# A weight converter that runs four steps further ahead in a fused attention and expert-layer kernel

## The chip, the cores and the metric

One core of one Trainium2 chip. The metric is the device time of one execution in microseconds: 653.36 us, the median of three runs (652.16 to 654.46).

## The reference

Three layers, one behind the other, all in float32:

```
attention: q, k, v of (2, 8, 576, 64); scores = q k^T / 8, masked per head:
           heads 0-3 see the last 32 positions, heads 4-7 every 32nd position
           attn = softmax(scores); x = attn v, as (1152, 512)
dense:     x = ((x @ w1) * (x @ w2)) @ w3 @ w_out      (512 -> 1024 -> 1024 -> 512)
experts:   p = probs / (sum(probs) + 1e-9); out = sum over 4 experts e of
           p[:, e] * (relu(x @ u1[e]) @ u2[e])         (512 -> 1024 -> 512)
```

The dense weights w1, w2, w3 and w_out arrive as float64, 8 bytes an element.

## The kernel before, in words

**Products.** Each factor is split into a high and a low part, and every product is three matmuls (`mm3`, L256 to L258): high by high, low by high, high by low. A weight chunk is thus of use only when both `w_hi` and `w_lo` of it exist; the third matmul of a block is the first that reads `w_lo`.

**Weight conversion.** The 20 chunks of the dense weights (8 of w1 and w2 together, 4 of w_out, 8 of w3) come as 64-bit words and are turned into float32 by integer work on the two 32-bit halves (class `Chunk`, L124 on): `round_up` (ScalarE, L136) works on the low words, `magnitude` (ScalarE, L144; for chunk 0 VectorE, L142) takes the high words without their sign into a tile `t`, then `clamp` (L147), `shift` (L150), `sign` (L153) and `add` (L157) on VectorE; `add` joins the low words and its method issues the load of the next raw chunk on SyncE's queue, with further loads hung on some of them (`rest_loads`: the third carries v of batch 1, the fourth its q and k, the fifth more of v). Last, `split_hi` (ScalarE, L164) writes w_hi and `split_lo` (VectorE, L174) writes w_lo. There are two raw buffers and two `t` tiles, so chunk n+2 is loaded when `add` of chunk n is done.

**Who hands the steps out.** The generator `work()` (L201) lists these steps in order and yields between them; `advance(n)` takes n of them. The engines work their queues in the order in which the program issues instructions, so where `advance` stands between other work is where the steps stand in each engine's queue. `split_hi` waits, by not being issued, while `live`, the count of occupied tiles of the pool for values and weights, is over 14. `need(chunk)` takes steps until that chunk is split.

**Stages.** Attention of batch 0 is nine steps of `attend(0, s)` with `advance` of 2, 3, 1 and 1 steps behind steps 4 to 7, which is just chunk 0 as far as its w_lo, and some idle matmuls (`keep_warm`). Then come 32 units, `run_unit()`: batch 0, then batch 1; in each, 8 feature groups (ft), each needing weight chunk ft, by 2 halves of the tokens. A unit is two accumulators of 12 matmuls (`ab_block`): the first is copied by ScalarE (L476), the second multiplied by that copy on VectorE (L478), and behind each stands `advance(1)`. Attention steps of batch 1 (`attend(1, s)`, nine of them) stand behind units 2, 4, 5, 7, 8, 10, 11, 13 and 14, and free value tiles as they go. Batch 1 uses the same eight chunks and frees them one by one. Behind the units: w3 times w_out in eight tiles (`wc_tile`, accumulators `wc_acc`), each needing one more chunk, with `advance(5)` behind each; x3, the dense layer's output; and the experts.

**Pools.** Five PSUM banks serve all accumulators except the scores and the experts' products, which have three of their own.

Of the kernel before, what the change touches and what calls it, by code (L numbers as in the profile page):

```python
# [42 lines left out]
def kernel(  # L43
# [157 lines left out]
    def work():  # L201


        wide = stream[:20]
        wide[0].round_up()
        wide[0].magnitude()
        yield True
        before = None
        for c, after in zip(wide, wide[1:] + [None]):
            if before:  # L210
                while live > 14:
                    yield False
                before.split_hi()
            c.clamp()
            yield True
            if before:
                before.split_lo()
            c.shift()
            yield True
            c.sign()  # L220
            yield True
            if after:
                after.round_up()
            c.add()
            yield True
            before = c
            if c is wide[0]:
                c.split_hi()
                yield True
                c.split_lo()  # L230
                yield True
                before = None
            if after:
                after.magnitude()
        while live > 14:
            yield False
        before.split_hi()
        yield True
        before.split_lo()
        yield True  # L240
        for w in c_e:
            yield from w.work()

    worker = work()

    def advance(n=1):

        return all([next(worker, False) for _ in range(n)])
# [363 lines left out]
    class Step:  # L612
# [22 lines left out]
        def add(self, out, acc, b):  # L635
            nc.vector.tensor_tensor(out=out, in0=acc, in1=b, op=ALU.add)  # L636

        def first(self, work):

            n = self.half.n  # L640
# [6 lines left out]
            self.product(b, "s2", "t2")  # L647
            self.add(u2, b, u1)
            work(1)
            self.product(c, "s3", "t3")  # L650
            self.add(u3, c, u2)
# [69 lines left out]
    with tc.manual_schedule():  # L721
# [42 lines left out]
        def attend(b, s):  # L764

            nonlocal live
            chunk = chunks[b]
            n = len(chunk)
            if s == 0:
                chunk[0].scores()  # L770
            if s + 1 < n:
                chunk[s + 1].scores()
            if s < n:
                chunk[s].maxima()
                chunk[s].exps()
            if 1 <= s <= n:
                chunk[s - 1].sums()
                chunk[s - 1].normalise()
            if 3 <= s:
                c = chunk[s - 3]  # L780
                c.pv()
                c.put()
                c.put_lo()
                if c.g == 0 or c.c > 0:
                    live -= 1
            if 2 <= s < n + 2:
                chunk[s - 2].transposes()
                chunk[s - 2].evac(nc.scalar.copy)

        for s in range(9):  # L790
            attend(0, s)
            advance({4: 2, 5: 3, 6: 1, 7: 1}.get(s, 0))
            keep_warm({4: 20, 5: 14, 6: 12, 8: 16}.get(s, 8))
        steps = iter(range(9))
        while done < 16:
            run_unit()
# [13 lines left out]
        for it in range(8):  # L810
# [9 lines left out]
            if i is not None:  # L820
                c = wc[i]
# [4 lines left out]
        c = None  # L826
# [134 lines left out]
```

## Time and profile before

| | |
|---|---|
| median of three runs | 653.36 us (652.16 to 654.46) |
| the profiled execution | 652.93 us, of which its span is 651.1 |
| TensorE busy | 626.3 us, 96% of the span |
| VectorE busy | 454.3 us, 70% |
| ScalarE busy | 265.0 us, 41% |
| mean granted TensorE clock | 0.990 |

Engines are named PE (TensorE matmuls), PEld (its weight loads), DVE (VectorE), ACT (ScalarE), POOL (GpSimd) and SP (SyncE). Times in a timeline are from the first instruction of the span. What stands in square brackets behind an instruction is the time that its engine was idle just before it, and what ended that. Back-to-back instructions overlap by about a tenth of a microsecond in their records. The clock is given as a share of full speed.

### The profile page before, as it was taken

The page shows a single profiled execution, that of the slowest core. Times are in us where ns is not written, and L with a number is a line of the kernel's source. Part 1 is how long each engine was busy: PE and PEld are TensorE (multiplying, and loading weights), DVE is VectorE, ACT ScalarE, POOL GpSimd, SP SyncE. Part 2 cuts the span into 40 slices and gives each one's busy share as a digit, 9 for nine tenths or more (in the row PEclk, how much of TensorE's full clock was granted, in tenths as well). Part 3 has the DMA queues.
Part 4 walks back from the last instruction along what each step waited for, and adds up shares of the span by engine and source line. Part 5 has one row for each costly group of instructions (what it writes and reads, how often), then busy time and mean ns, then how long its engine had stood idle before and what let it go on. Part 6 is the DMA issues. An engine that isn't in the chain of part 4 may idle for free.

```text
span 651.1 us, 11452 instructions
## 1 busy us (share of the span) xinstructions
PE 626.3 (96%) x4706; PEld 571.1 (88%) x4706; DVE 454.3 (70%) x819; ACT 265.0 (41%) x455; POOL 4.9 (1%) x25
## 2 busy tenths in 40 slices
PE   8879896999998999999999999999899999999997
PEld 6778796999886999999899989998798989899996
DVE  5956797489877512677787787797786575664843
ACT  3634464466664412433343343334434333333321
POOL 2000000000000000000000000000000000000000
PEclk9989899999999999999999999999999999999999
DMA  8854323234333311143355335543568564656311
GB/s 261 301 163 125 119 72 125 66 99 158 133 130 129 130 65 65 35 150 139 130 193 182 143 134 190 182 142 130 193 214 319 195 225 163 211 188 246 131 65 65
DMA packets 28727, 99.45 MB, mean 153 GB/s; under 512 B 2652, under 2 KB 6740, under 8 KB 26116
## 3 DMA queue, kind: packets, MB, share of 16 engines
q1 hardware_dynamic: 28132, 98.14, 42.8%
q8 instruction: 37, 0.61, 0.4%
q10 hardware_dynamic: 544, 0.59, 0.3%
q14 instruction: 14, 0.11, 0.0%
HBM read 79.58 MB, written 19.14 MB: 152 GB/s over the span
## 4 chain that ended last, share of the span: by engine, by line
PE 75%; DVE 11%; DMA 6%; ACT 5%; issue 2%; SPq 0%; DVEq 0%; ACTq 0%
PE g_acc L256 10%; PE g_acc L257 10%; PE g_acc L258 10%; PE m_a L256 4%; PE m_a L258 4%; PE m_a L257 4%; DMA raw<-in_w3T_dram 3%; PE ab_acc L258 3%; PE ab_acc L256 3%; PE ab_acc L257 3%; PE x_acc L256 3%; PE x_acc L257 3%; PE x_acc L258 3%; PE m_b L257 3%; PE m_c L256 3%; PE m_c L257 3%
## 5 line engine op out<-in xcount | busy, mean ns | idle before, releaser
L630 ACT ACTIVATE h_hi<-u 128x320 fp32r<-128x320 f32 (+1 forms) x128 | 57.0, 446 | 188.4 <-DVE u L636 188.4
L256 PE MATMUL g_acc<-w_hi,h_hi 128*128 128x512 f32 (+1 forms) x296 | 114.3, 386 | 0.0
L257 PE MATMUL g_acc<-w_lo,h_hi 128*128 128x512 f32 (+1 forms) x296 | 114.2, 386 | 0.0
L258 PE MATMUL g_acc<-w_hi,h_lo 128*128 128x512 f32 (+1 forms) x296 | 113.7, 384 | 0.0
L256 PE MATMUL ab_acc<-x_hi,w_hi 128*128 128x288 f32 x256 | 79.5, 311 | 7.9 <-ACT w_hi L164 7.9
L258 PE MATMUL ab_acc<-x_hi,w_lo 128*128 128x288 f32 x256 | 78.7, 307 | 4.8 <-DVE w_lo L174 4.8
L257 PE MATMUL ab_acc<-x_lo,w_hi 128*128 128x288 f32 x256 | 77.9, 304 | 0.0
L636 DVE TENSOR_TENSOR u<-m_b,u 128x320 f32<-128x320 f32 (+1 forms) x96 | 40.8, 453 | 53.1 <-PE m_b L258 51.4
L569 DVE TENSOR_TENSOR w_lo<-raw,w_hi 128x768 fp32r<-128x768 f32 x64 | 69.4, 1085 | 12.0 <-ACT w_hi L567 11.9
L258 PEld LDWEIGHTS g_acc<-w_hi,h_lo 128*128 128x128 f32 x296 | 55.6, 188 | 11.6
L256 PEld LDWEIGHTS g_acc<-w_hi,h_hi 128*128 128x128 f32 x296 | 55.8, 188 | 8.0
L257 PEld LDWEIGHTS g_acc<-w_lo,h_hi 128*128 128x128 f32 x296 | 55.7, 188 | 7.6
L632 DVE SCALAR_TENSOR_TENSOR h_lo<-u,h_hi 128x320 fp32r<-128x320 f32 (+1 forms) x128 | 57.8, 451 | 3.5 <-ACT h_hi L630 1.4
L567 ACT CAST w_hi<-raw 128x768 fp32r<-128x768 f32 x64 | 59.9, 936 | 0.0
L256 PEld LDWEIGHTS ab_acc<-x_hi,w_hi 128*128 128x128 f32 x256 | 50.6, 197 | 9.3 <-ACT w_hi L164 8.6
L258 PEld LDWEIGHTS ab_acc<-x_hi,w_lo 128*128 128x128 f32 x256 | 50.4, 197 | 6.5 <-DVE w_lo L174 6.3
L257 PEld LDWEIGHTS ab_acc<-x_lo,w_hi 128*128 128x128 f32 x256 | 50.6, 198 | 0.0
L257 PE MATMUL m_b<-b_t,s_hi 128*128 128x320 f32 (+1 forms) x128 | 37.9, 296 | 0.0
L636 DVE TENSOR_TENSOR u<-m_a,u 128x320 f32<-128x320 f32 (+1 forms) x64 | 28.9, 452 | 11.6 <-PE m_a L258 11.6
L569 DVE TENSOR_TENSOR s_lo<-raw,s_hi 128x1024 fp32r<-128x1024 f32 x16 | 19.6, 1225 | 23.2 <-ACT s_hi L567 23.2
L636 DVE TENSOR_TENSOR u<-m_c,u 128x320 f32<-128x320 f32 (+1 forms) x64 | 29.0, 453 | 4.6 <-PE m_c L258 3.8
L136 ACT ACTIVATE raw<-raw 128x1024 int32<-128x1024 uint32 x20 | 23.4, 1170 | 20.7 <-DMA raw<-in_w3T_dram 18.3
(153 smaller groups left out, 1388.2 us busy)
## 6 DMA issues: line engine op xcount, KB each, us to landing
raw<-in_e_dram SPq DMA_DIRECT2D x32, 1024.0 KB
raw<-in_w_dram SPq DMA_DIRECT2D x8, 1024.0 KB
raw<-in_w3T_dram SPq DMA_DIRECT2D x8, 1024.0 KB
stored<-s_hi SPq DMA_DIRECT2D x16, 512.0 KB
stored<-s_lo SPq DMA_DIRECT2D x16, 512.0 KB
s_hi<-stored SPq DMA_DIRECT2D x16, 512.0 KB
s_lo<-stored SPq DMA_DIRECT2D x16, 512.0 KB
raw<-in_w_out_dram SPq DMA_DIRECT2D x4, 1024.0 KB
```

Source lines behind the costliest of these rows:

```text
L136: nc.scalar.activation(self.low, self.low.bitcast(U32), AF.Copy, scale=2.0 ** -29)
L256: mm(acc, lh, rh, start=first, stop=False)
L257: mm(acc, lh, rl, start=False, stop=False)
L258: mm(acc, ll, rh, start=False, stop=last)
L567: nc.scalar.copy(dst[0], src)
L569: nc.vector.tensor_tensor(out=dst[1], in0=src, in1=dst[0].bitcast(F32), op=ALU.subtract)
L630: nc.scalar.activation(hi, src, AF.Relu)
L632: nc.vector.scalar_tensor_tensor(out=lo, in0=src, scalar=0.0, in1=hi.bitcast(F32), op0=ALU.max, op1=ALU.subtract)
L636: nc.vector.tensor_tensor(out=out, in0=acc, in1=b, op=ALU.add)
```

## The change

Two edits. In `work()`, the `round_up` of chunk 1 moves from ahead of `add` of chunk 0 to behind `split_hi` of chunk 0, in the step that issues that; its `magnitude` stays where it was. For every later chunk `magnitude` moves from behind the yield that follows `add` of the chunk before to directly behind `round_up`, ahead of that `add`. In the main program four more steps are handed out between the attention of batch 0 and the first unit: `magnitude` and `clamp` of chunk 1; `shift`; `sign`; `round_up` and `magnitude` of chunk 2 with `add` of chunk 1 and the loads behind it.

```
             c.sign()
             yield True
-            if after:
+            if after and c is not wide[0]:
                 after.round_up()
+                after.magnitude()
             c.add()
             yield True
             before = c
             if c is wide[0]:
                 c.split_hi()
+                after.round_up()
                 yield True
                 c.split_lo()
                 yield True
                 before = None
-            if after:
                 after.magnitude()
...
             attend(0, s)
             advance({4: 2, 5: 3, 6: 1, 7: 1}.get(s, 0))
             keep_warm({4: 20, 5: 14, 6: 12, 8: 16}.get(s, 8))
+        advance(4)
         steps = iter(range(9))
         while done < 16:
             run_unit()
```

## Rows read from the trace of the kernel before

**Rows 1.** The profile's page, busy us (share of the span) and instructions of each engine.
```profile
PE 626.3 (96%) x4706; PEld 571.1 (88%) x4706; DVE 454.3 (70%) x819; ACT 265.0 (41%) x455; POOL 4.9 (1%) x25
```

**Rows 2.** TensorE's waits, 215 to 651: us in total, times, longest.
```profile
PE m_a L256 <- ACT u L646: 0.9, 1, 0.9
```

**Rows 3.** TensorE's waits, 33 to 109.
```profile
PE ab_acc L256 <- ACT w_hi L164: 6.3, 3, 3.3
PE ab_acc L258 <- DVE w_lo L174: 3.9, 5, 1.5
```

**Rows 4.** TensorE's timeline at two waits: start, us, line, form [idle before].
```profile
45.15 0.61 PE L256 MATMUL ab_acc<-x_hi,w_hi 128*128 128x288 f32 x1 [3.31 <-ACT w_hi L164]
46.41 0.61 PE L258 MATMUL ab_acc<-x_hi,w_lo 128*128 128x288 f32 x1 [0.41 <-DVE w_lo L174]
...
67.32 0.40 PE L256 MATMUL ab_acc<-x_hi,w_hi 128*128 128x288 f32 x1 [2.05 <-ACT w_hi L164]
```

**Rows 5.** Stretches: length, PE, PEld, DVE, ACT, POOL busy; clock; DMA share, GB/s.
```profile
36.03:39.36 3.33, 3.33 (x28) 3.33 (x26) 2.77 (x4) 1.58 (x3) 0.00 (x0) 1.00 0.00 0
33.40:109.15 75.75, 65.49 (x844) 60.33 (x842) 56.25 (x94) 35.52 (x60) 0.23 (x2) 0.93 0.37 121
46.81:51.61 4.80, 4.80 (x21) 4.80 (x21) 1.37 (x2) 1.44 (x2) 0.00 (x0) 0.50 0.52 196
68.61:72.05 3.44, 3.44 (x15) 3.44 (x16) 1.77 (x2) 0.67 (x2) 0.00 (x0) 0.52 0.03 5
80.00:98.00 18.00, 17.29 (x225) 15.91 (x217) 17.44 (x32) 10.90 (x23) 0.00 (x0) 1.00 0.22 65
113.14:116.50 3.36, 3.36 (x16) 3.36 (x15) 1.27 (x2) 1.43 (x2) 0.00 (x0) 0.50 0.02 5
```

**Rows 6.** TensorE's waits, 109 to 126.
```profile
PE ab_acc L256 <- ACT w_hi L164: 1.6, 1, 1.6
PE ab_acc L258 <- DVE w_lo L174: 0.9, 1, 0.9
```

**Rows 7.** ScalarE's timeline at the end of batch 0's attention.
```profile
27.70 1.05 ACT L164 CAST w_hi<-t 128x1024 fp32r<-128x1024 f32 x1 [1.06 <-DVE t L157]
28.65 0.90 ACT L437 CAST x_hi<-o 128x216 fp32r<-128x216 f32 x2
29.94 0.59 ACT L389 COPY pT<-tp 128x512 f32<-128x512 f32 x1 [0.39 <-PE tp L384]
31.60 0.68 ACT L437 CAST x_hi<-o 128x108 fp32r<-128x108 f32 x4 [1.07 <-PE o L410]
```

**Rows 8.** ScalarE's instructions by line, 33.4 to 109.15: busy us, mean ns; idle before.
```profile
L144 ACT ACTIVATE t<-raw 128x1024 f32<-128x1024 f32 x8 | 9.1, 1137 | 0.0
L136 ACT ACTIVATE raw<-raw 128x1024 int32<-128x1024 uint32 x7 | 8.2, 1166 | 0.0
```

**Rows 9.** VectorE's instructions by line, the same stretch.
```profile
L153 DVE SCALAR_TENSOR_TENSOR t<-raw,t 128x1024 int32<-128x1024 int32 x7 | 8.6, 1222 | 0.1
L157 DVE CUSTOM_DVE_ANT_0 t<-raw,t 128x2048 uint16<-128x2048 uint16 x7 | 8.5, 1216 | 0.0
...
L147 DVE TENSOR_SCALAR t<-t 128x1024 f32<-128x1024 f32 x7 | 4.9, 694 | 8.6 <-ACT t L144 8.6
```

**Rows 10.** A stretch, columns as in rows 5.
```profile
41.55:50.00 8.45, 4.72 (x38) 4.21 (x28) 4.70 (x6) 3.25 (x5) 0.00 (x0) 0.69 0.77 263
```

**Rows 11.** The chain that ended last, in order of time: start, us, what.
```profile
165.69 5.87 DMA raw<-in_w3T_dram
```

**Rows 12.** VectorE's waits, 126 to 206.
```profile
DVE t L147 <- ACT t L144: 6.7, 8, 1.6
```

**Rows 13.** TensorE's waits, 130 to 240.
```profile
PE wc_acc L256 <- ACT w_hi L164: 1.3, 1, 1.3
PE wc_acc L258 <- DVE w_lo L174: 0.8, 1, 0.8
```

**Rows 14.** ScalarE's timeline in batch 1.
```profile
128.18 0.40 ACT L476 COPY ab<-ab_acc 128x288 f32<-128x288 f32 x1 [0.62 <-PE ab_acc L258]
```

More of the change, by code (lines that the diff above doesn't have):

```diff
@@ L221, in work @@
             yield True
-            if after:
+            if after and c is not wide[0]:
                 after.round_up()
+                after.magnitude()
             c.add()
@@ L228, in work @@
                 c.split_hi()
+                after.round_up()
                 yield True
@@ L232, in work @@
                 before = None
-            if after:
                 after.magnitude()
@@ L793 @@
             keep_warm({4: 20, 5: 14, 6: 12, 8: 16}.get(s, 8))
+        advance(4)
         steps = iter(range(9))
```

## The prediction

> **What bounds the kernel now.** I read the page's busy line first, then TensorE's waits stage by stage, its timeline at the waits, and last the other engines' queues at the same places. TensorE is busy 626.3 us (96%) [rows 1], so what can be won is some 25 us of waits and whatever it runs at the low clock. Behind 215 us there is next to nothing: the longest wait there is 0.9 us [rows 2]. The place to look is the first projection of batch 0, from the end of its attention (33.4) to the end of batch 1's (109.15). There TensorE waits 6.3 us in 3 waits for w_hi and 3.9 us in 5 for w_lo [rows 3]: at the turn from one eighth of the features (ft) to the next, the weight chunk is not yet converted. The largest are 3.31 + 0.41 us before ft 1 and, for w_hi alone, 2.05 before ft 3 [rows 4]. Behind each of these two the granted clock is 0.50 and 0.52, the lower of the two levels (1.2 GHz) [rows 5]. One more wait of this kind stands at ft 7, 1.6 + 0.9 us [rows 6], also with a stretch at 0.50 behind it [rows 5].
>
> Why it waits is in the order of the code. Two converter steps go with each half of a batch's tokens, so the chunk for ft k is split in the last unit of ft k-1, and its w_lo stands on VectorE behind the product of that unit's last accumulator. TensorE has always finished before. For ft 1 it is worse, since none of chunk 1's four steps is out before the first block.
>
> **The change part by part.**
>
> *The round_up of chunk 1 goes behind split_hi of chunk 0.* ScalarE runs that split at 27.70, the next x_hi copies at 28.65, the pT copy at 29.94 for 0.59 us [rows 7]. A round_up has a mean of 1.17 us [rows 8], some 1.07 back to back. With it in between, the x_hi copies begin at about 29.7 and, at 0.90, the pT copy at 30.6 or a little later, so the last attention product, and ft 0 behind it, begin 0.6 us later. The slot that the round_up leaves, earlier in the same loop, gives nothing back: the VectorE chain there does not wait for it. Cost 0.6; between 0, if the 16 idle matmuls ahead of ft 0 took it up, which they can't as they stand in TensorE's queue behind that product, and the whole 1.17.
>
> *Four steps before the first block.* They issue on ScalarE a magnitude (1.14), a round_up (1.17) and another magnitude; on VectorE clamp 0.69, shift (an estimate: as the clamp), sign 1.22 and add 1.22 [rows 8, 9]; and behind the add on SyncE the load of raw chunk 3 and, since that load carries them, the q and k of batch 1. ScalarE is through with the attention's last copies at 31.60 + 0.68 [rows 7], 32.9 with the shift of 0.6. So: magnitude to 34.0, clamp, shift, sign, add to 37.8, w_hi to 38.9. Clamp 2 and the first product come in VectorE's queue ahead of w_lo, which is done at about 40.1. TensorE came to these weights at 45.15 - 3.31 = 41.84 [rows 4], now 42.4. Both are there 2 us before. Behind the waiting instructions, ScalarE's first copy of an accumulator (wanted at 35.6) stands until about 36.5 and VectorE's first product until 38.7; that holds two of five PSUM banks, and TensorE needs the first of them again only at 44. No cost. The wait of 3.7 us goes, and with it the slow stretch: 20 matmuls start from 46.81 to 51.61 (21 are counted, one reaches in), 0.24 us each. At full clock 25 start in 3.33 us (28 counted, three reach in), 0.133 each; 20 would take 2.7 us, so 2.1 us go too [rows 5].
>
> *The lead stays.* From now on each chunk is split in the first unit of the ft before, a whole unit earlier (24 matmuls of 0.133, 3.2 us, and an attention step). That covers the other waits up to ft 6: 10.2 - 3.7 = 6.5 us, and the slow stretch of ft 3, 3.44 - 14 x 0.133 = 1.6 us (15 counted, one reaches in) [rows 5]. So all that goes is 10.2 + 2.1 + 1.6 = 13.9 us, and TensorE alone would need 75.75 - 13.9 + 0.6 = 62.5 us. VectorE has 56.25 us to do in the stretch [rows 5], 90% of that. It can be driven so hard: from 80 to 98 it was busy 17.44 of 18 us with TensorE at full clock [rows 5]. But it will now often be the one that is late, and TensorE then waits for the PSUM banks of x_lo and of products. Bounds: nothing, and 4 us (a quarter of the cover of 3.2 us lost at each of five turns); I take 1.5.
>
> *The load moved ahead.* In the kernel before, the DMA engines are at work for the 8.45 us from the issue at 41.55, on 1 MB of raw and 1.15 MB of q and k [rows 10]; a raw load by itself takes up to 5.87 us [rows 11]. Issued now at 37.8, raw 3 lands at 42.7 to 46.3. ScalarE comes to its round_up near 39, so this is a new wait of 3.7 to 7 us, and behind it stand magnitude 3, the first exp of batch 1, the copy of ft 1's first accumulator and split_hi 2. With 42.7, w_lo 2 is ready near 48 and TensorE wants it at 49.9: free. With 46.3 it comes at 51.5: 1.6 us. The nearer row is a raw load by itself, as it is issued first. The Trainium skill (DMA: Bandwidth & Descriptors, "Two DMAs through the same engine are not ordered") says that descriptors of one queue start in order but are pipelined and that nothing orders DMAs across the 16 engines; by that the raw load could end with the others. No run here shows its own landing; the sum would be 1.6 us worse.
>
> *At ft 7 nothing changes.* There is room for w_hi and w_lo of chunk 7 only when the last values of batch 1 are freed (live > 14), in both kernels after the same attention step, so 2.5 us [rows 6] and the slow stretch stay. From here the steps handed out are the same as before, and the lead is at an end: what was won by then is kept as a shift.
>
> *Magnitude directly behind the low words, all later chunks.* It moves past one or two ScalarE copies of an accumulator. While TensorE sets the pace that is free either way. In batch 1 and the weight product behind it VectorE waits 6.7 us in 8 clamps for a magnitude [rows 12], and the converter is late in the end: TensorE waits 1.3 us for w_hi and 0.8 for w_lo [rows 13]. Part of those 6.7 us goes, since w_lo (via split_hi behind the delayed copies) takes some of it back. Bounds: nothing won, or 2.1 us; below nothing too, by 1 us, since the copy of an accumulator now stands 1.04 us longer behind a late load. I take 1.1, the middle of the first two.
>
> **The sum.** 13.9 - 0.6 - 1.5 + 1.1 = 12.9 us. The profiled execution took 652.93 us (span 651.1), 0.4 below the median of the three runs, 653.36. 652.93 - 12.9 = 640.0 us.
>
> **The rivals.**
> *The converter doesn't move.* From 134 to 206 the chain of waits runs through raw loads and conversions, with loads of up to 5.87 us in it [rows 11], not through TensorE. If that chain kept its place, TensorE would come 13 us early to the seventh tile of the weight product and wait there: 652. If half of it moved, 646.5. Against it: the chain starts anew in batch 1, when chunk 0's room is freed, and ScalarE's copy ahead of that first split had waited for TensorE, 0.62 us [rows 14]. So it starts when TensorE lets it.
> *VectorE becomes the bound.* If half of the 6.5 us of waits behind ft 1 come back, at TensorE's banks instead of its weights, and the clock drops at two of them (2 x 1.6), the gain is 12.9 - 3.3 - 3.2 = 6.4: 646.5. For it: 90% load in a queue that must keep its order. Against: the stretch from 80 to 98.
> *Slower: the lower clock for most of the stretch.* With VectorE saturated, TensorE could wait a little at each accumulator and stay at 1.2 GHz from ft 1 to ft 6. A unit of 24 matmuls then takes 24 x 0.107 = 2.6 us more. The gain of 12.9 is gone at 5 units of the 12; at 8 units the time is 640 + 20.8 = 661. For it: a stretch at 0.50 behind each of three waits. Against: from 80 to 98 the clock was 1.00 beside a VectorE at 97%. The Trainium skill (TensorE: Matmul & The Clock Gate, "A second HAM failure mode: psum-queue depth-cycling") describes just this, a kernel that idles briefly between groups of matmuls as it goes round its PSUM banks and has its clock fall and rise; by that rule the time would be the 661 above, and the trace so far doesn't bear it out.
> *It doesn't do what it says:* the four steps only push the first block's copies back, and the wait before ft 1 moves to ft 0. Then the start costs 0.6 and the waits stay: 653.5. The 2 us of room worked out above speak against it.
>
> **How the numbers follow.** Forecast 72%, VectorE bound 13%, converter in part 6% and not at all 2%, lower clock 5%, not done 2%. The forecast's own range: best 13.9 - 0.6 + 2.1 + 1.5 (no slow stretch at ft 7) = 16.9, so 636; worst 13.9 - 0.6 - 4 - 1.6 - 1 = 6.7, so 646.2. With 0.4 for the spread of the runs I give 635.8 to 646.8, which takes in the second rival and half of the third. Faster by over 0.3% (about what a measurement of this kernel can tell): the first three and most of the fourth, 0.92; within 0.3%: 0.03; slower: 0.05.
>
> **What would show it.** Right: no wait for w_hi or w_lo before ft 1, and a clock of 1.00 from 42 to 52; ft 0 starts near 34.0; the last attention product of batch 1 ends near 98 instead of 109.15; VectorE busy over 85% between; the wait of 2.5 us at ft 7 still there; the wait at the seventh weight tile shorter than 2.1 us; behind it everything shifted alike. Wrong: waits of accumulators for x_lo or products that add up to over 4 us; the lower clock in more than two of ft 2 to ft 6; a wait at the seventh tile longer than before.

## The result, and the profile after

The changed kernel took 637.96 us (median, 637.03 to 639.57) beside 653.91 for the kernel before on the same chip: a ratio of 0.9761, 95% interval 0.9728 to 0.9793. By that ratio it takes 15.6 us less (13.5 to 17.8). The span of its profiled execution is 635.4 us against 651.1. The program has one line more, so L256 to L258 are L257 to L259 now.

First TensorE's waits, from the profile of the changed kernel, in the three stretches that answer to [rows 3], [rows 6] and [rows 13] (us in total, times, longest):

```profile
PE ab_acc L257 <- ACT pT L390: 1.0, 1, 1.0
PE o L411 <- ACT pT L390: 0.6, 1, 0.6
...
PE ab_acc L257 <- ACT w_hi L164: 1.6, 1, 1.6
PE ab_acc L259 <- DVE w_lo L174: 0.9, 1, 0.9
...
PE wc_acc L259 <- DVE w_lo L174: 0.8, 1, 0.8
```

Between 33 and 97 no wait for w_hi or w_lo is left; two short waits for pT have taken their place. The wait at ft 7 stands as it was. At the seventh tile of the weight product the wait for w_hi (1.3) is gone, the one for w_lo is not.

Then stretches of the changed kernel, with the columns of [rows 5]: all of the first projection of batch 0 up to the end of batch 1's attention, the place of the first slow stretch of before, and the place behind ft 7.

```profile
34.70:95.72 61.02, 59.43 (x846) 56.23 (x844) 56.23 (x94) 34.79 (x60) 0.23 (x2) 1.00 0.46 154
42.00:52.00 10.00, 10.00 (x178) 9.30 (x167) 8.87 (x12) 4.92 (x7) 0.00 (x0) 1.00 0.88 321
98.00:102.00 4.00, 3.19 (x13) 3.20 (x14) 2.95 (x4) 0.34 (x2) 0.00 (x0) 0.58 0.01 4
```

The same stretch of before, from its first matmul, is the next row: the same 846 matmuls and the same 56.2 us of VectorE.

```profile
33.18:109.15 75.97, 65.71 (x846) 60.55 (x843) 56.25 (x94) 35.52 (x60) 0.23 (x2) 0.93 0.38 122
```

It has shrunk by 14.95 us, of which 8.7 are TensorE's idle time (10.3 to 1.6) and 6.3 its busy time. The rest of the path shows in where the next stages begin. The matmuls of the first projection (`ab_acc`, which begins with ft 0), of the weight product (`wc_acc`) and of x3 (`x_acc`), before and then after (min/median/max ns, first and last start us):

```profile
L256 PE MATMUL ab_acc<-x_hi,w_hi x256: 288/295/607, 33.2 to 170.9; 128*128 128x288 f32 x128
L256 PE MATMUL wc_acc<-w_hi x64: 387/389/501, 171.7 to 217.5; 128*128 128x512 f32 x64
L256 PE MATMUL x_acc<-ab_hi,w_hi x96: 290/295/297, 218.2 to 267.8; 128*128 128x288 f32 x96
```

```profile
L257 PE MATMUL ab_acc<-x_hi,w_hi x256: 288/294/442, 34.7 to 157.3; 128*128 128x288 f32 x128
L257 PE MATMUL wc_acc<-w_hi x64: 389/389/494, 157.7 to 201.9; 128*128 128x512 f32 x64
L257 PE MATMUL x_acc<-ab_hi,w_hi x96: 290/295/297, 202.6 to 252.3; 128*128 128x288 f32 x96
```

The shift is +1.5 at ft 0, -13.6 where TensorE ends the first projection (170.9 to 157.3), -14.0 where the weight product begins, -15.6 at x3, and -15.7 at the end of the span. Behind the start of x3 it changes by no more than 0.1. Of the +1.5, 1.2 came with this execution and not with the change: add of chunk 0 already starts that much later (26.44 before, 27.60 after), behind a first raw load that took 6.83 us in the chain of waits where it took 5.07 before. From the start of that add to the end of the span the two profiles differ by 16.9 us (624.7 and 607.8).

### The profile page after: what moved, and what is told of

Read it like the earlier page. It is cut to its first block, busy times and chain, and to the rows that moved or that the text cites. A ratio compares the mean times of both kernels' runs of the same rounds, so it can differ in the third digit from the quotient of the medians.

```text
span 635.4 us, 11454 instructions
## 1 busy us (share of the span) xinstructions
PE 620.3 (98%) x4706; PEld 567.2 (89%) x4706; DVE 453.9 (71%) x819; ACT 264.8 (42%) x455; POOL 5.0 (1%) x25
## 4 chain that ended last, share of the span: by engine, by line
PE 79%; DMA 8%; DVE 6%; ACT 5%; issue 1%; SPq 0%; DVEq 0%
PE g_acc L257 10%; PE g_acc L258 10%; PE g_acc L259 10%; DMA raw<-in_w3T_dram 5%; PE m_a L257 4%; PE m_a L259 4%; PE m_a L258 4%; PE ab_acc L257 3%; PE ab_acc L259 3%; PE ab_acc L258 3%; PE x_acc L259 3%; PE x_acc L257 3%; PE x_acc L258 3%; PE m_b L258 3%; PE m_c L257 3%; PE m_c L258 3%
## 5 line engine op out<-in xcount | busy, mean ns | idle before, releaser
L257 PE MATMUL g_acc<-w_hi,h_hi 128*128 128x512 f32 (+1 forms) x296 | 114.3, 386 | 0.0
L258 PE MATMUL g_acc<-w_lo,h_hi 128*128 128x512 f32 (+1 forms) x296 | 114.2, 386 | 0.0
L259 PE MATMUL g_acc<-w_hi,h_lo 128*128 128x512 f32 (+1 forms) x296 | 113.7, 384 | 0.0
L257 PE MATMUL ab_acc<-x_hi,w_hi 128*128 128x288 f32 x256 | 77.1, 301 | 2.7 <-ACT w_hi L164 1.6
L259 PE MATMUL ab_acc<-x_hi,w_lo 128*128 128x288 f32 x256 | 76.3, 298 | 0.9 <-DVE w_lo L174 0.9
L258 PE MATMUL ab_acc<-x_lo,w_hi 128*128 128x288 f32 x256 | 76.0, 297 | 0.0
L259 PEld LDWEIGHTS g_acc<-w_hi,h_lo 128*128 128x128 f32 x296 | 55.6, 188 | 11.6
L257 PEld LDWEIGHTS g_acc<-w_hi,h_hi 128*128 128x128 f32 x296 | 55.8, 188 | 8.0
L258 PEld LDWEIGHTS g_acc<-w_lo,h_hi 128*128 128x128 f32 x296 | 55.7, 188 | 7.6
L257 PEld LDWEIGHTS ab_acc<-x_hi,w_hi 128*128 128x128 f32 x256 | 48.7, 190 | 3.5 <-ACT w_hi L164 1.7
L259 PEld LDWEIGHTS ab_acc<-x_hi,w_lo 128*128 128x128 f32 x256 | 48.7, 190 | 1.2 <-DVE w_lo L174 1.2
L258 PEld LDWEIGHTS ab_acc<-x_lo,w_hi 128*128 128x128 f32 x256 | 48.6, 190 | 0.0
L258 PE MATMUL m_b<-b_t,s_hi 128*128 128x320 f32 (+1 forms) x128 | 37.9, 296 | 0.0
```

The lines of the kernel that those rows point to most:

```text
L257: mm(acc, lh, rh, start=first, stop=False)
L258: mm(acc, lh, rl, start=False, stop=False)
L259: mm(acc, ll, rh, start=False, stop=last)
```

## The experiments

**The four steps alone, and the order alone.** Two parts make the change. In e1 the kernel before got only this line:

```
+        advance(4)
         steps = iter(range(9))
```

> The kernel before with the four early steps alone; every magnitude and the round_up of chunk 1 stay where they were. Theory (the gain is the waits for weights and the slow clock behind them; the earlier magnitude takes VectorE's waits for it and helps a converter that is late): most of the gain, 641 to 645, no wait for w_hi or w_lo before ft 1 to ft 6, and a longer wait at the seventh weight tile than in the changed kernel (0.8 us). Rival 1, the place of the magnitude is free: 638, as the changed kernel. Rival 2, the place of the magnitude is most of it: 647 or more.

It took 642.72 us, 0.9815 of the kernel before (0.9777 to 0.9854). In e2 the changed kernel lost that line and kept the rest:

```
-        advance(4)
         steps = iter(range(9))
```

> The changed kernel without the four early steps: only the magnitudes directly behind the low words, and round_up of chunk 1 behind split_hi of chunk 0. Theory: the wait of some 3 us before ft 1 and its slow stretch stay; VectorE waits less, 648 to 651. Rival 1, the place of the magnitude is free: 653.5. Rival 2, it is most of the gain: 643 or less.

It took 647.76 us, 0.9897 (0.9859 to 0.9936), a little better than I had given it. So the steps alone are worth some 12 us and the order alone some 7, where both together are worth 15.6. Whether the two overlap is not shown: the intervals are too wide for it, and in the profiles, from add of chunk 0 to the end, the parts give 9.0 and 5.9 us and both together 16.9. The steps are not the whole and the order is not free: e2's interval lies clear of 1, and the changed kernel's ratio lies outside e1's interval. But the two intervals of e1 and of the changed kernel touch (0.9777 to 0.9793), so what the order adds to the steps rests on the profiles more than on the time. TensorE's waits show what each leaves; e1 first, from 126 to 230, and with it a stretch behind those waits (columns of [rows 5]):

```profile
PE wc_acc L256 <- ACT w_hi L164: 1.8, 1, 1.8
PE wc_acc L258 <- DVE w_lo L174: 0.8, 1, 0.8
...
198.10:201.50 3.40, 3.40 (x9) 2.63 (x8) 2.46 (x3) 0.84 (x1) 0.00 (x0) 0.50 0.00 0
```

Without the order, the converter is as late at the seventh weight tile as before, even a little later, and in this profile the lower clock follows. (It is the longest of e1's four executions, 644.49 us at a mean clock of 0.991; the shortest took 640.80 at 0.997.) In e2, from 33 to 106:

```profile
PE ab_acc L259 <- DVE w_lo L174: 3.9, 5, 2.1
PE ab_acc L257 <- ACT w_hi L164: 3.7, 3, 2.3
```

The waits for weights are still there, 7.6 us against the 10.2 of before. VectorE waits 3.7 us for one magnitude in this stretch, against 8.6 in 6 before; that this is why the weights come sooner is the likely reading, not one tested by itself. The seventh tile waits only the 0.8 us of the changed kernel.

The two profiles also show what the order does behind the first projection, from its last block to the start of x3; e1, then e2:

```profile
L256 PE MATMUL ab_acc<-x_hi,w_hi x256: 288/294/442, 33.8 to 160.4; 128*128 128x288 f32 x128
L256 PE MATMUL x_acc<-ab_hi,w_hi x96: 290/295/297, 209.7 to 259.4; 128*128 128x288 f32 x96
...
L257 PE MATMUL ab_acc<-x_hi,w_hi x256: 288/295/609, 33.8 to 167.2; 128*128 128x288 f32 x128
L257 PE MATMUL x_acc<-ab_hi,w_hi x96: 290/295/297, 212.4 to 262.1; 128*128 128x288 f32 x96
```

From 160.4 to 209.7 are 49.3 us in e1, from 167.2 to 212.4 are 45.2 in e2; before it was 47.3, and the changed kernel has 45.3. So the order gains 2 us there without any lead, and without the order the lead loses 2 of what it had won, for the most part in the 3.4 us at half the clock.

**The clock by itself.** Were the slow stretches behind the two long waits worth anything beside the waits? In e4 the kernel before runs idle matmuls in them:

```
                 attend(1, next(steps))
+            keep_warm({2: 28, 6: 17}.get(done, 0))
```

> The kernel before with 28 idle matmuls in TensorE's wait before ft 1 and 17 in the one before ft 3, so that TensorE is busy there; no weight comes earlier. Theory (the slow stretches behind the two waits cost 2.1 + 1.6 us of the gain on top of the waits): the clock stays at 1.00 behind both, 649 to 651. Rival, the slow stretches are hidden beside VectorE's work or the clock falls all the same: 653 to 654.

650.97 us, 0.9929 (0.9904 to 0.9954): 4.6 us (3.0 to 6.3) less, though no step of the converter is handed out sooner. The two places, with the columns of [rows 5]:

```profile
42.00:52.00 10.00, 9.11 (x154) 7.70 (x153) 7.57 (x10) 3.94 (x5) 0.00 (x0) 1.00 0.51 169
68.00:74.00 6.00, 5.04 (x45) 4.20 (x43) 4.34 (x6) 2.49 (x4) 0.00 (x0) 1.00 0.18 75
...
31.00:37.00 6.00, 6.00 (x56) 4.26 (x55) 2.96 (x8) 1.20 (x5) 0.00 (x0) 0.50 0.76 265
```

The clock is at 1.00 behind both, and the gain agrees with the 3.7 us worked out for them. The third row is a stretch at the lower clock that this profile has ahead of ft 0, where the kernel before had none; so the profile itself doesn't show the gain, only the timed runs do.

**How far ahead.** e8 hands out two steps, e7 eight:

```
-        advance(4)
+        advance(2)      # e8
+        advance(8)      # e7
```

> The changed kernel with two early steps in place of four: each chunk is split in the second unit of the ft before, behind the product of its last accumulator, as in the kernel before. Theory (the whole unit of lead is what covers the waits): the wait before ft 1 goes, as attention scores stand between, but those before ft 3 and ft 6, where nothing stands between, come back with some 2 us each, 640 to 645. Rival, any lead will do: 638.

> The changed kernel with eight early steps in place of four, so round_up of chunk 3 also stands ahead of the first block, and waits for its load there. Theory (what counts is what stands behind the waiting instruction): ScalarE can't copy the first accumulators until some 45, TensorE runs out of PSUM banks in ft 0 or ft 1 and the clock may fall, 641 to 645. Rival, more lead covers more waits: 636 to 638.

e8 took 641.66 us, 0.9840 (0.9802 to 0.9879), as the theory has it. In its timeline the waits are back where no scores stand between two fts:

```profile
59.86 0.40 PE L257 MATMUL ab_acc<-x_hi,w_hi 128*128 128x288 f32 x1 [1.03 <-ACT w_hi L164]
61.28 0.40 PE L259 MATMUL ab_acc<-x_hi,w_lo 128*128 128x288 f32 x1 [0.89 <-DVE w_lo L174]
...
88.57 0.40 PE L257 MATMUL ab_acc<-x_hi,w_hi 128*128 128x288 f32 x1 [0.33 <-ACT w_hi L164]
91.22 0.54 PE L259 MATMUL ab_acc<-x_hi,w_lo 128*128 128x288 f32 x1 [2.11 <-DVE w_lo L174]
```

The first two are before ft 3, the others before ft 6. So it is the whole unit of lead that covers them. e7 took 645.53 us, 0.9891 (0.9864 to 0.9917): more lead is worse. Its ScalarE:

```profile
43.26 1.14 ACT L136 ACTIVATE raw<-raw 128x1024 int32<-128x1024 uint32 x1 [4.05 <-DMA raw<-in_w_dram]
...
45.29 0.39 ACT L477 COPY ab<-ab_acc 128x288 f32<-128x288 f32 x1
...
51.00 1.15 ACT L136 ACTIVATE raw<-raw 128x1024 int32<-128x1024 uint32 x1 [4.08 <-DMA raw<-in_w_dram]
```

The first copy of an accumulator of ft 0 stands behind the wait for raw 3 and comes at 45.29. I expected TensorE to run out of PSUM banks there, and it did, but for 1.22 us only. The larger price was paid later, and the lower clock followed it (the second row has the columns of [rows 5]):

```profile
62.04 0.90 PE L385 MATMUL tp<-ident,p_pair 128*128 128x128 f32 x3 [5.13 <-DVE p_pair L380]
...
62.04:67.13 5.09, 5.09 (x22) 5.09 (x23) 4.95 (x10) 1.66 (x5) 0.11 (x1) 0.50 0.34 142
```

VectorE reached the normalised scores of batch 1 only at 61.43, and TensorE's transpose waited 5.13 us for them. Ahead of them in VectorE's queue stood the conversion steps handed out early, which had themselves waited 1.83 and 0.91 us for magnitudes behind the two late loads. So the place was only partly what I had said: the price comes through what is queued behind a waiting instruction, but in part simply through four more steps that stand ahead of the attention; the runs don't part the two.

**The moved round_up.** e3 puts chunk 1's round_up back ahead of add of chunk 0:

```
-            if after and c is not wide[0]:
+            if after:
                 after.round_up()
+            if after and c is not wide[0]:
                 after.magnitude()
...
                 c.split_hi()
-                after.round_up()
```

> The changed kernel with round_up of chunk 1 back ahead of add of chunk 0; the rest as changed. Theory: behind split_hi it delays the last attention product, and so ft 0, by 0.6 us; back in its old place ft 0 starts 0.4 to 0.6 us sooner after add of chunk 0 and all behind it shifts alike, 637.5. Rival, it is needed where it is: add of chunk 0 waits for it or VectorE's order there suffers, 638 to 640.

636.44 us, 0.9751 (0.9716 to 0.9787), whose interval covers the changed kernel's 0.9761: the time doesn't settle it. The profiles do. In e3 ft 0 starts 6.73 us after the start of add of chunk 0 (26.04 to 32.77), as before (26.44 to 33.18), where the changed kernel needs 7.13 (27.60 to 34.74). With the old place e1, e10 and e11 also give 6.73 or 6.74; with the new one e2, e6, e7 and e9 give 7.13 to 7.16, and e8 7.35. (e4 had the lower clock in this place.) So the move costs 0.4 us, and no gain from it shows.

**Room for chunk 7.** The wait at ft 7 was put down to room alone. e6 lets batch 1's attention end one unit sooner, e9 two:

```
-            if done in (2, 4, 5, 7, 8, 10, 11, 13, 14):
+            if done in (2, 4, 5, 7, 8, 10, 11, 12, 13):      # e6
+            if done in (2, 4, 5, 7, 8, 9, 10, 11, 12):       # e9
```

> The changed kernel with the last two attention steps of batch 1 behind units 12 and 13 in place of 13 and 14, so that the room for chunk 7 is free one unit earlier. Theory (the wait at ft 7 is for room alone, and the conversion is ready): the waits of 1.6 + 0.9 us before ft 7 and the slow stretch behind them go, 634 to 635.5. Rival, VectorE is then late with the attention step or with chunk 7, and the wait moves to unit 13 or stays: 637 to 639.

> The changed kernel with the last four attention steps of batch 1 behind units 9, 10, 11 and 12, so that the room for chunk 7 is free before unit 12. Theory: the 1.6 us wait for w_lo of chunk 7 that was left with the room free at unit 13 goes too, 632 to 633.5. Rival, VectorE can't keep up with an attention step behind each of five units, and TensorE waits there instead: 634.5 or more.

e6 took 634.43 us, 0.9697 (0.9663 to 0.9730), e9 633.11, 0.9709 (0.9675 to 0.9743). In e6 the wait for w_hi and the slow stretch are gone, and 1.6 us for w_lo are left:

```profile
96.92 0.40 PE L259 MATMUL ab_acc<-x_hi,w_lo 128*128 128x288 f32 x1 [1.56 <-DVE w_lo L174]
```

In e9 that too is gone. What its waits from 33 to 126 still have are two for pT:

```profile
PE o L402 <- ACT pT L390: 1.0, 1, 1.0
PE o L411 <- ACT pT L390: 0.9, 1, 0.9
```

e6 has such waits too, 1.0 and 0.6 us. So e6 shows that the wait for w_hi was for room, and e9 that the one for w_lo goes as well when the room comes two units sooner. The two ratios can't be told apart. Last, both with the round_up back, in five rounds each:

> Both that helped together: round_up of chunk 1 back ahead of add of chunk 0, and the last two attention steps behind units 12 and 13. Theory (the two lie at different places of TensorE's path and add up): 0.4 us below the second alone, 0.967 to 0.970 of the kernel before. Rival, they don't add: 0.972 or more.

> The same with the last four attention steps behind units 9 to 12. Theory (the wait for w_lo of chunk 7 goes, but new waits for transposes and pT of about the same size take its place, as the attention steps crowd): the same as with units 12 and 13 within 1 us. Rival, it is faster by the whole 1.6 us of that wait.

e10 took 633.08 us, 0.9696 (0.9668 to 0.9724), e11 632.46, 0.9662 (0.9637 to 0.9687). The two intervals overlap, and neither is told apart from e6 or e9. All four ratios lie below the changed kernel's, those of e10 and e11 with their whole intervals below its interval; e11 is the version I would keep. By the time it is not shown that the round_up adds to them, nor which of the two expectations for e11 holds. The profiles speak against the first of these, that new waits take the place of the one for w_lo: from the start of ft 0 to the end of the span they take 598.5 us in e6 and 598.3 in e10, and 596.8 in e9 and 597.0 in e11, so 1.4 to 1.7 less with the room two units sooner.

## Why the prediction was right

It said 640.0 us and a gain of 12.9; the time was 637.96 and the gain 15.6. The mechanism held. The sum fell short because the waits were worth more than their rows said, and the magnitudes too. (With the 0.4 for the spread, the terms of the range give 635.6 to 646.6, not 635.8 to 646.8; nothing rests on it.) Step by step:

- *The waits before ft 1 to ft 6 go, and with them the slow stretches.* So it was; the clock from 42 to 52 is 1.00. e4 shows the clock's part by itself, e8 that the lead of a whole unit is what does it.
- *The size of that term was too small.* I gave 13.9 us less 1.5 of new waits. The new waits came to 1.6, yet the stretch shrank by 14.95, and 13.9 - 1.6 = 12.3 of it leaves 2.6. A wait costs more than the idle time put down to it. In the changed kernel's timeline:

```profile
72.88 0.30 PE L259 MATMUL ab_acc<-x_hi,w_lo 128*128 128x288 f32 x1
...
74.15 0.40 PE L257 MATMUL ab_acc<-x_hi,w_hi 128*128 128x288 f32 x1 [0.98 <-ACT pT L390]
74.39 0.30 PE L258 MATMUL ab_acc<-x_lo,w_hi 128*128 128x288 f32 x1
```

From the start ahead of the wait to the second start behind it are 1.51 us; two steps of 0.133 would be 0.27; so 1.24 are lost where the row says 0.98. The last matmul runs out (0.30 against a step of 0.133), and the first one behind holds up the next for 0.24. The kernel before shows the same: from 56.29 over a wait of 0.71 us to 57.53 are 1.24 us, 0.26 more than the wait and two steps. With 0.26 a wait, the eight waits of before [rows 3] cost 2.1 us more than their 10.2; the two new waits cost some 0.5 more in the same way, which leaves 1.6. Another 0.3 is the matmuls at 45.15 and 46.41 [rows 4], which ran at the lower clock already and were left out of the slow stretch: 0.40 to the next start, where 0.24 is usual behind a wait. And some 0.45 are two short hold-ups of before, at 81.0 to 81.4 and 84.1 to 84.6, for which no idle time is shown. Some 0.3 stays open.
- *The start of ft 0 is 0.6 us later.* 0.4, by the profiles of e3 and of the change.
- *Raw 3 lands at 42.7 to 46.3, and ScalarE waits 3.7 to 7 us without harm.* SyncE's issue and ScalarE's wait in the changed kernel:

```profile
38.86 0.35 SPq L132 DMA_DIRECT2D raw<-in_w_dram  x1
...
43.92 1.15 ACT L136 ACTIVATE raw<-raw 128x1024 int32<-128x1024 uint32 x1 [3.68 <-DMA raw<-in_w_dram]
```

The load landed 5.06 us after its issue: the nearer end, a load by itself. What the Trainium skill says there (DMA: Bandwidth & Descriptors, "Two DMAs through the same engine are not ordered"), that nothing orders DMAs across the 16 engines, did not show in this landing. TensorE lost nothing by it. The next load, issued at 44.57 with loads of v behind it, was waited for until 51.30, 6.73 us, also without a wait of TensorE.
- *VectorE becomes the limit only in part.* It was busy 56.23 of 61.02 us, 92%, and TensorE's new waits came to 1.6 us, against 1.5. So the second rival fell. But they came at another place than I had said: not at the banks of x_lo or of products, but for ScalarE's copy of pT, which stood behind an exp that had waited 2.03 us (and before the second wait 2.46) for VectorE:

```profile
72.72 0.57 ACT L366 ACTIVATE p_pair<-p_pair 128x432 f32<-128x432 f32 x1 [2.03 <-DVE p_pair L360]
73.20 0.52 ACT L438 CAST x_hi<-o 128x192 fp32r<-128x192 f32 x2
73.60 0.49 ACT L390 COPY pT<-tp 128x384 f32<-128x384 f32 x1
```

VectorE was late, as said; that the size fitted so well was luck, since the 1.5 was picked between nothing and 4.
- *Nothing changes at ft 7.* The same 1.6 + 0.9 us, and a slow stretch behind them (0.58). That it was room, e6 and e9 show.
- *The later magnitudes give 1.1 us.* They gave 2.0: from the end of the first projection to x3 the shift grows from 13.6 to 15.6, and in e2, which has no lead, the same stretch is 2.1 shorter than before. In the profiles VectorE's waits for magnitudes, 6.7 us before [rows 12], are down to 1.1, and 3.2 us of that came back as waits for ab_hi. I had said that w_lo would take some of it back; its waits grew by 0.3 only. VectorE's waits, before from 126 to 206, then the changed kernel from 112 to 192:

```profile
DVE w_lo L174 <- ACT w_hi L164: 5.7, 4, 3.2
DVE ab_lo L484 <- ACT ab_hi L482: 0.5, 1, 0.5
DVE ab_lo L455 <- ACT ab_hi L454: 0.4, 2, 0.2
...
DVE w_lo L174 <- ACT w_hi L164: 6.0, 4, 3.2
DVE ab_lo L456 <- ACT ab_hi L455: 2.2, 2, 2.0
DVE ab_lo L485 <- ACT ab_hi L483: 1.9, 2, 1.4
DVE t L147 <- ACT t L144: 1.1, 1, 1.1
```

What I didn't say is what e2 shows: this edit helps in the first projection too, where the waits for weights are 2.6 us shorter by it alone. I had counted those waits as all gone by the lead, so it changed nothing in the sum.
- *The converter moves with TensorE.* In the changed kernel it did, so the first rival fell. In e1 it did not quite: with the steps alone 2 us of the lead were lost again behind the first projection. The order, which I had entered as a small gain of its own, also keeps what the steps win.
- *The lower clock stays.* From ft 1 to ft 6 the clock was 1.00 throughout, so the slower rival fell, and with it, for this kernel, the rule of the Trainium skill named there (TensorE: Matmul & The Clock Gate, "A second HAM failure mode: psum-queue depth-cycling"). In e1, which waits a little longer in the same places, a stretch at the lower clock did appear: from 85 to 90, behind a wait of 1.55 us for pT, the row is

```profile
85.00:90.00 5.00, 5.00 (x28) 5.00 (x28) 4.51 (x9) 4.07 (x9) 0.00 (x0) 0.66 0.11 44
```

## What to carry to other kernels

Where one engine prepares what another consumes and both keep program order, a stall at each turn can be a question of where the steps are handed out: work out behind which instruction of the consumer's block the last step stands, and give it a lead of a whole block. A step further ahead also brings its load's wait ahead, and what is queued behind that wait pays: of the three leads tried here four steps were best, two too few and eight too many. Then look at the next place where the converter may be late: here the lead kept its worth behind the first projection only together with the earlier magnitudes. And count a wait of TensorE as its idle time plus the run-out, the restart and any slow stretch behind it; here 10.2 us of waits were worth about 16 (an estimate: 10.2 + 2.1 + 3.7).

## What was not expected of the hardware

A wait of TensorE cost 0.26 us more than the idle time shown for it. Where the lower clock came was not told by the length of the single wait: 3.7 us in two pieces before ft 1 and 2.5 at ft 7 were each followed by it, while 0.91 + 1.51 before ft 6 of the kernel before was not; but 0.33 + 2.11 at the same place in e8 was (0.50 from 91.4 to 94.7), and so was 1.55 in e1. Why one and not the other stays open. With idle matmuls in the two long waits the lower clock did not follow them (e4).
